# Moving the slot arithmetic of eight pairs of units from VectorE to GpSimd, in a delta-rule attention and mixture-of-experts kernel

## Chip, cores and metric

One core of one Trainium2 chip. The metric is the device time of one execution in microseconds; three runs of the kernel before gave 531.09, 531.88 and 532.16 us, median 531.88 us.

## What is computed

Two stages, in float32. The first is linear attention with a delta rule, for 4 batches and 8 heads, 768 time steps, head dimension 48:

```python
for t in range(S):
    y[:, :, t] = einsum('bhd,bhde->bhe', q[:, :, t], state)
    v_old = einsum('bhde,bhd->bhe', state, k_n[:, :, t])
    state = state + beta_t * einsum('bhd,bhe->bhde', k_n[:, :, t], v[:, :, t] - v_old)
```

The second takes the 3072 rows of that output (384 wide) through a top-1 mixture of 8 experts:

```python
logits = x @ w_gate
expert_idx = argmax(logits, axis=1)          # the first of equals
gate_w = softmax(logits)[arange(N), expert_idx]
out[row] = gate_w[row] * (relu(x[row] @ w1[e]) @ w2[e])   # e = expert_idx[row]
```

## The kernel before

The sequence is cut into 6 blocks of 128 steps; a block of one batch is a **unit**, so there are 24 units, numbered n = 6 blocks x 4 batches in the order in which they are finished. The first part of the kernel is a pipeline over stages t = 0 to 26. In a stage, four units are in flight, each with another quarter of its 128 rows.

The order of the instructions is written out by hand (the program is traced with a manual schedule, and each engine does its instructions in that order). One stage does this:

- `residual(t)`: TensorE multiplies states and earlier corrections (L395, L407) into `ks`, and VectorE subtracts `ks` from the values `v_all` (L414).
- `apply(t)`: TensorE multiplies `v_all` with the inverse of a triangular matrix (L422), and ScalarE copies the result to `u` (L426).
- `finish(n)` for the unit n = t - 3: TensorE starts the output `yp` (L445), makes the state's increment `ku` (L454), VectorE adds it to the state (L458), TensorE completes `yp` (L463), ScalarE copies it to `yt` (L467). In the stage after that, `emit_x` transposes the unit's output into rows of tokens and gate logits (L487 on TensorE, L488 on ScalarE, L489 on VectorE).
- Between these, `beside(t, 0)` to `beside(t, 6)` issue other work, seven portions in a stage: steps of the triangular inverses of later blocks (VectorE, L355 and L359, a product into `tmp` and a subtraction from `lw`, alternating), and steps of the slot arithmetic below, 3, 3, 3, 2, 2, 2 and 2 in the seven portions. The first three portions lie between L414 and L458 of a stage, the other four behind L458.
- `qpart(n)` makes the masked products `pm`: TensorE (L260), two copies by ScalarE (L270), then GpSimd's AFFINE_SELECT over 1024 columns (L271), once in a stage.

**Slot arithmetic** (`emit_slots`, L491 to L565). Two finished units form a pair (the last four units go one by one). Each token must learn its row in `xg`, a table in device memory where the tokens of an expert lie together. On the small arrays [128 tokens, 2 units, 8 experts] VectorE does: the row's maximum (L505), logits minus maximum into `row` (L508), a descending number where that is zero (L513), its maximum (L516), the one-hot `ohb` of the first of equals (L519). Ten steps later TensorE counts (L523, L526: a triangle of ones and ones times `ohb`, into `pp` in PSUM). Then VectorE does seven more: position (L529), the running count `base` (L531), overflow test (L539), its addition (L541), times one-hot (L543), sum over the experts into `sl_all` (L545), cast to integers `sli` (L553). SyncE writes the rows to `xn`, and GpSimd scatters the two units' rows to `xg` with two indirect transfers (L560). ScalarE copies two columns of token numbers into `row` (L511).

The number of the expert (`m2_all`, from L516) is used again only in the part for experts that overflow their 448 rows (L1102 on); in this data that part does not run, and no instruction of it is in the trace.

The second part of the kernel goes over the 8 experts (`ffn`): three products for each matmul (high and low halves of float32), TensorE nearly without a gap from 300 us to the end. The first expert's weights are loaded and split from stage 20 on, and half of its tokens are worked on in the last stages (`early`).

At the start, GpSimd makes constants (`constants()`, L75 to L97): masks, `rev_e`, `base`, `lim`, token numbers.

Of the kernel before, what the change touches and what calls it, by code (L numbers as in the profile page):

```python
# [8 lines left out]
F32 = mybir.dt.float32  # L9
F32R = mybir.dt.float32r  # L10
BF16 = mybir.dt.bfloat16
I32 = mybir.dt.int32
AF = mybir.ActivationFunctionType
ALU = mybir.AluOpType
AX = mybir.AxisListType
# [4 lines left out]
C = 128  # L20
NT = S // C
# [20 lines left out]
def deltanet_moe(ctx, tc, kt_d, qt_d, kn_d, v_d, beta_d, w_gate, w1, w2, out):  # L42
# [13 lines left out]
    ltri = cp.tile([128, 128], BF16, name="ltri")  # L56
    ones = cp.tile([128, 128], BF16, name="ones")
    rev_e = cp.tile([128, E], F32, name="rev_e")
    base = cp.tile([128, E], F32, name="base")
    lim = cp.tile([128, E], F32, name="lim")  # L60
    jump = cp.tile([128, 2, E], F32, name="jump")
# [1 line left out]
    kind_i = cp.tile([128, E], I32, name="kind_i")  # L63
    sl_all = cp.tile([128, B * NT], F32, name="sl_all")
    m2_all = cp.tile([128, B * NT], F32, name="m2_all")
    ids = cp.tile([128, B * NT], F32, name="ids")
    ids2 = cp.tile([128, B * NT, 2], F32, name="ids2")
    zrow = cp.tile([128, ROW], F32, name="zrow")
# [3 lines left out]
    def iota(t, pattern, start, step=0):  # L72
        nc.gpsimd.iota(t, pattern=pattern, base=start, channel_multiplier=step, allow_small_or_imprecise_dtypes=True)

    def constants():  # L75
        nc.gpsimd.memset(esel, 0.0)
        for p in range(NP):
            for a in range(2):

                r = slice(64 * a, 64 * a + D)  # L80
                nc.gpsimd.tensor_copy(esel[r, p, (p + a) % 2 * D:((p + a) % 2 + 1) * D], ident[r, r])
        cmask = lp.tile([128, 128], F32, name="cmask", tag="u", bufs=UB)
        nc.gpsimd.memset(cmask, 1.0)
        nc.gpsimd.affine_select(out=cmask, in_=cmask, compare_op=ALU.is_gt, fill=0.0, base=0,
                                pattern=[[1, 128]], channel_multiplier=-1)
        nc.gpsimd.tensor_copy(ltri, cmask)
        nc.gpsimd.memset(ones, 1.0)
        iota(last_i, [[1, CAP - 128 * NG]], 128 * NG)
        iota(rev_e, [[-1, E]], E)
        iota(base, [[CAP, E]], 0)  # L90
        iota(lim, [[CAP, E]], CAP)
        nc.gpsimd.memset(jump, 0.0)
        for i, g in enumerate((G0, NG)):
            nc.gpsimd.memset(jump[:, i, 0:1], float(128 * g))
        iota(ids, [[-C, B * NT]], int(TOPID), -1)
        nc.gpsimd.memset(ids2, 0.0)
        nc.gpsimd.tensor_copy(ids2[:, :, 0], ids)  # L97
        wv = w_gate.rearrange("(p a r) e -> a r p e", p=NP, a=2)
        for a in range(2):
            for o in range(2):  # L100
                nc.sync.dma_start(out=esel[64 * a:64 * a + D, o::2, 2 * D:], in_=wv[(a + o) % 2, :, o::2])
# [30 lines left out]
    DM2 = 0  # L132
    DEF = 2
    FP = 10
    AH = 3
    TOK = (0, 5, 8, 9, 10)
    PC = (1, 3, 4, 6, 8, 9, 11)
# [82 lines left out]
    def kpart(n):  # L220

        tb, b = n // B, n % B
        kt, gg = kt_t[n] if n < KTL else kg_t[n % KTG], gg_t[n % KSL]
        V, A = nc.vector.tensor_copy, nc.scalar.copy
        if tb == 0:
            if n == 0:
                tiles["dg"] = fp.tile([128, BH, 32], F32, name="dg")
            dg = tiles["dg"]
            db = [psg_[-1].tile([128, NP, 32], F32, name=f"db{b}_0", tag="g"),
                  pss.tile([128, NP, 32], F32, name=f"db{b}_1", tag="y", bufs=YB)]  # L230
            for h in range(H):
                p, a = h // 2, h % 2
                r = slice(64 * a, 64 * a + 64)
                for i in range(NB):
                    t = slice(32 * i, 32 * i + 32)
                    nc.tensor.matmul(db[a][t, p, :], lhsT=kt[r, p, t], rhs=kt[r, p, t], start=True, stop=True,
                                     tile_position=(64 * a, 32 * i), skip_group_check=True)
            V(out=dg[:, b * H:(b + 1) * H:2], in_=db[0])
            A(out=dg[:, b * H + 1:(b + 1) * H:2], in_=db[1])
            yield  # L240
        pg = halves(f"pg{tb}_{b}", kt, kt)
        for a in range(2):
            A(out=gg[:, a:H:2], in_=pg[a])  # L243
        if tb > 0 and b == B - 1:
            for i in range(NB):
                r = slice(32 * i, 32 * i + 32)
                nc.sync.dma_start(out=gd[tb].rearrange("(i n) (r c) -> i r n c", i=NB, r=32)[i],
                                  in_=gg_g[tb % (KSL // B)].rearrange("p b h c -> p (b h) c")[r, :, r])
            tiles[tb]["lg"] = fp.tile([128, 32, 32], F32, name=f"lg{tb}", tag="lg", bufs=3)
            nc.sync.dma_start(out=tiles[tb]["lg"].rearrange("p r c -> p (r c)"), in_=gd[tb])  # L250
        if n >= KTL:
            load_g(n + KTG)
# [177 lines left out]
    def finish(n):  # L430

        tb, b = n // B, n % B
        last = tb == NT - 1
        st, u = st_t[b], uview(n)
        qt, pm = qt_t[n % QTL], pm_t[n % QSL]
        yp = [pss.tile([128, NP // 2, C], F32, name=f"yp{tb}_{b}_0", tag="y", bufs=YB),
              psg_[-1].tile([128, NP // 2, C], F32, name=f"yp{tb}_{b}_1", tag="g")]

        def place(h, m):
            o = 64 * ((h // 2 + h) % 2)  # L440
            return yp[h // 2 % 2][o:o + m, h // 4, :]

        for h in range(H):
            r = slice(64 * (h % 2), 64 * (h % 2) + 64)
            nc.tensor.matmul(place(h, 64), lhsT=st[r, h // 2, r], rhs=qt[r, h // 2, :], start=(h < 4), stop=True,  # L445
                             tile_position=(r.start, 64 * ((h // 2 + h) % 2)), skip_group_check=True)
        yield
        if not last:
            ku = pss.tile([112, NP, D], F32, name=f"ku{tb}_{b}", tag="y", bufs=YB)
            for h in range(H):  # L450

                m = 64 if h % 2 == 0 else D
                kn = tiles[tb][b]["kn"].rearrange("t h d -> t (h d)")[:, h * D:h * D + m]
                nc.tensor.matmul(ku[64 * (h % 2):64 * (h % 2) + m, h // 2, :], lhsT=kn, rhs=u[:, h, :],  # L454
                                 start=True, stop=True, skip_group_check=True)
            for a in range(2):
                r = slice(64 * a, 64 * a + D)
                nc.vector.tensor_tensor(out=st[r, :, r], in0=st[r, :, r], in1=ku[r], op=ALU.add)  # L458
            if n + NB_ < NN - B:
                load_ku(n + NB_)  # L460
        yield
        for h in range(H):
            nc.tensor.matmul(place(h, D), lhsT=u[:, h, :], rhs=pm[:, h, :],  # L463
                             start=False, stop=True, skip_group_check=True)
        yt = lp.tile([128, NP, C], F32, name=f"yt{tb}_{b}", tag="yt", bufs=2)
        for o in range(2):
            nc.scalar.copy(out=yt[:, o::2], in_=yp[o])  # L467
        yield
        w = 1 if n >= NN - W1 else 2
        if n % w == 0:  # L470
            tiles["row", n // w, w] = (rp if n < NN - 2 else xq_[0]).tile([128, 2 if n < NN - 2 else 1, ROW], F32, name=f"row{tb}_{b}", tag="row", bufs=2)
            tiles["rl", n // w, w] = lp.tile([128, 2, E], F32, name=f"rl{tb}_{b}", tag="rl", bufs=2)
        row, rl = tiles["row", n // w, w], tiles["rl", n // w, w]
        row, rl = row[:, 0:w], rl[:, 0:w]
        emit_x(n, yt, row[:, n % w], rl[:, n % w])
        if n % w == w - 1:
            fine.append(emit_slots(tb, b - w + 1, w, row, rl))

    def st_view(b, p):
        t = st_t[b][:, p, :]  # L480
# [10 lines left out]
    def emit_slots(tb, b, w, row, rl):  # L491
# [3 lines left out]
        def small(nm, shape, dt=F32):  # L495
            return lp.tile(shape, dt, name=f"{nm}{tb}_{b}", tag=f"{nm}{w}", bufs=2)
# [15 lines left out]
        oh = small("oh", [128, w, E])  # L512
        V.scalar_tensor_tensor(out=oh, in0=lm, scalar=0.0, in1=both(rev_e), op0=ALU.is_ge, op1=ALU.mult)  # L513
        yield
        m2 = m2_all[:, cols]
        V.tensor_reduce(out=m2, in_=oh, axis=AX.X, op=ALU.max)  # L516
        yield
        ohb = small("ohb", [128, w, E], BF16)
        V.tensor_tensor(out=ohb, in0=oh, in1=wide(m2), op=ALU.is_ge)  # L519
        for _ in range(FP if w > 1 else 3):  # L520
            yield
# [41 lines left out]
            load_main(0, 0, G0)  # L563
        if tb * B + b + w == NN - DEF:
            load_main(0, G0, NG)  # L565

    def run(gen, steps=1):

# [534 lines left out]
    def small(nm, shape=(128, E), dt=F32):  # L1103
        return op.tile(list(shape), dt, name=nm)
# [8 lines left out]
    tsi = small("tsi", (128, B * NT), I32)  # L1113
    nc.vector.tensor_scalar(out=tm, in0=sl_all, scalar1=BIG, scalar2=-BIG, op0=ALU.is_ge, op1=ALU.mult)
    nc.vector.tensor_tensor(out=ts_, in0=sl_all, in1=tm, op=ALU.add)
    nc.vector.tensor_scalar(out=tm, in0=m2_all, scalar1=-float(N - CAP), scalar2=float(E * (N - CAP)),
                            op0=ALU.mult, op1=ALU.add)
    nc.vector.tensor_tensor(out=ts_, in0=ts_, in1=tm, op=ALU.add)
# [123 lines left out]
```

## Time and profile before

| | |
|---|---|
| median of 3 runs | 531.88 us (531.09 to 532.16) |
| the profiled execution: its time / its span | 529.1 us / 527.4 us |
| granted TensorE clock, mean over the span | 0.949 of full speed |
| TensorE matmul busy | 468.1 us (89%) |
| VectorE busy | 350.7 us (66%) |
| ScalarE busy | 268.4 us (51%) |
| GpSimd busy | 97.0 us (18%) |

The span runs from the first to the last instruction of the profiled execution; the 1.7 us between span and time lie outside of it. Busy times are unions: two overlapping instructions of an engine are counted once. In the busy map, VectorE is at nine tenths or more from 50 to 210 us in nearly every slice, and TensorE from 280 us on.

### The profile page before, as it was taken

The page shows a single profiled execution, that of the slowest core. Times are in us where ns is not written, and L with a number is a line of the kernel's source. Part 1 is how long each engine was busy: PE and PEld are TensorE (multiplying, and loading weights), DVE is VectorE, ACT ScalarE, POOL GpSimd, SP SyncE. Part 2 cuts the span into 40 slices and gives each one's busy share as a digit, 9 for nine tenths or more (in the row PEclk, how much of TensorE's full clock was granted, in tenths as well). Part 3 has the DMA queues.
Part 4 walks back from the last instruction along what each step waited for, and adds up shares of the span by engine and source line. Part 5 has one row for each costly group of instructions (what it writes and reads, how often), then busy time and mean ns, then how long its engine had stood idle before and what let it go on. Part 6 is the DMA issues. An engine that isn't in the chain of part 4 may idle for free. (4 is left out here: it accounts for less than half of the span.)

```text
span 527.4 us, 17531 instructions
## 1 busy us (share of the span) xinstructions
PE 468.1 (89%) x7212; PEld 429.8 (81%) x7212; DVE 350.7 (66%) x1135; ACT 268.4 (51%) x614; POOL 97.0 (18%) x125
## 2 busy tenths in 40 slices
PE   6866678998869888988889999999999999999995
PEld 4755667887758766877679889999999999999995
DVE  3999998899998999736654386636372837445330
ACT  2542346877747565755644255635354636344320
POOL 7001012033222212313230211020202020110202
PEclk9976879999998897998999999999999999999999
DMA  5878789588595654594452156655373746453001
GB/s 139 214 259 232 240 223 289 134 237 230 127 272 160 188 150 143 180 287 128 152 155 75 66 170 206 186 166 164 114 226 116 214 126 208 140 163 108 33 2 44
DMA packets 66061, 87.88 MB, mean 167 GB/s; under 512 B 26426, under 2 KB 50768, under 8 KB 65969
## 3 DMA queue, kind: packets, MB, share of 16 engines
q1 hardware_dynamic: 62512, 77.01, 49.8%
q0 software_dynamic: 3456, 9.57, 5.0%
q8 instruction: 67, 1.10, 0.9%
q14 instruction: 26, 0.20, 0.1%
HBM read 60.24 MB, written 23.56 MB: 159 GB/s over the span
## 5 line engine op out<-in xcount | busy, mean ns | idle before, releaser
L668 PE MATMUL y<-w2h,hx 128*128 128x384 f32 x352 | 94.2, 342 | 0.4 <-PEq L1041 0.4
L593 DVE TENSOR_TENSOR w2l<-w2r,w2h 128x768 fp32r<-128x768 f32 x32 | 31.3, 981 | 70.0 <-ACT w2h L592 69.7
L355 DVE TENSOR_TENSOR tmp<-lg,lw 128x192 f32<-128x192 f32 (+28 forms) x269 | 74.0, 310 | 2.8
L359 DVE TENSOR_TENSOR lw<-lw,tmp 128x192 f32<-128x192 f32 (+28 forms) x269 | 69.6, 294 | 0.5
L671 POOL DMA_INDIRECT out_dram<-yo,idx x32 | 30.6, 958 | 202.4 <-ACT yo L1014 129.0
L426 ACT COPY u<-ks 32x384 f32<-32x384 f32 x96 | 45.1, 470 | 39.3 <-PE ks L422 28.4
L668 PEld LDWEIGHTS y<-w2h,hx 128*128 128x128 f32 x352 | 64.2, 188 | 0.7 <-issue 0.7
L668 PE MATMUL y<-w2l,hx 128*128 128x384 f32 x176 | 59.5, 338 | 0.0
L657 PE MATMUL h<-xl,w1h 128*128 128x384 f32 (+1 forms) x168 | 57.6, 343 | 0.2 <-DVE xl L593 0.2
L657 PE MATMUL h<-xh,w1h 128*128 128x384 f32 (+1 forms) x168 | 57.6, 343 | 0.0
L657 PE MATMUL h<-xh,w1l 128*128 128x384 f32 (+1 forms) x168 | 57.5, 342 | 0.0
L271 POOL TENSOR_SCALAR_AFFINE_SELECT pm<-pm 128x1024 f32<-128x1024 f32 x24 | 27.3, 1138 | 130.0 <-ACT pm L270 130.0
L422 PE MATMUL ks<-v_all,wt 32*32 32x48 f32 x1536 | 28.7, 213 | 24.8 <-DVE v_all L414 22.2
L660 ACT ACTIVATE hx<-h 128x448 fp32r<-128x448 f32 (+1 forms) x64 | 32.8, 518 | 33.4 <-PE h L657 32.8
L395 PE MATMUL ks<-st,kt 128*32 128x96 f32 x768 | 46.7, 257 | 1.8 <-issue 1.8
L422 PEld LDWEIGHTS ks<-v_all,wt 32*32 32x32 f32 x1536 | 23.9, 112 | 29.7 <-DVE v_all L414 24.8
L661 DVE SCALAR_TENSOR_TENSOR hx<-h,hx 128x448 fp32r<-128x448 f32 (+1 forms) x64 | 37.0, 588 | 15.3 <-ACT hx L660 15.0
L1014 ACT ACTIVATE yo<-y,gt 128x384 f32<-128x384 f32 x21 | 12.2, 582 | 66.8 <-PE y L668 50.5
L243 ACT COPY gg<-pg 128x512 f32<-128x512 f32 x48 | 25.8, 588 | 32.6 <-PE pg L260 32.6
L395 PEld LDWEIGHTS ks<-st,kt 128*32 128x32 f32 x768 | 34.7, 113 | 5.5 <-issue 2.6
L560 POOL DMA_INDIRECT xg<-row,sli x24 | 26.1, 1089 | 69.1 <-DVE sli L553 39.8
L260 PE MATMUL pq<-qt,kt 64*128 64x128 f32 x384 | 32.3, 303 | 3.2 <-issue 1.9
(164 smaller groups left out, 955.0 us busy)
## 6 DMA issues: line engine op xcount, KB each, us to landing
w1r<-in_w_dram SPq DMA_DIRECT2D x24, 512.0 KB
w2r<-in_w_dram SPq DMA_DIRECT2D x32, 384.0 KB
kt<-in_kt_dram SPq DMA_DIRECT2D x24, 256.0 KB
qt<-in_qt_dram SPq DMA_DIRECT2D x24, 256.0 KB
xg<-zrow SPq DMA_DIRECT2D x7, 788.0 KB
kg<-in_kt_dram SPq DMA_DIRECT2D x17, 256.0 KB
xr<-xg SPq DMA_DIRECT2D x7, 591.0 KB
xn<-row SPq DMA_DIRECT2D x10, 394.0 KB
```

Of the source, the lines that this page charges most:

```text
L260: nc.tensor.matmul(pg[a][:, p], lhsT=kt[r, p], rhs=xt[r, p], start=True, stop=True, tile_position=(64 * a, 0), skip_group_check=True)
L355: nc.vector.tensor_tensor(out=x, in0=lg[:, r0:r1, c:c + 1].broadcast_to([128, r1 - r0, b - a]), in1=lw[:, c:c + 1, a:b].broadcast_to([128, ...
L359: nc.vector.tensor_tensor(out=lw[:, r0:r1, a:b], in0=lw[:, r0:r1, a:b], in1=x, op=ALU.subtract)
L395: nc.tensor.matmul(ks[32 * q:32 * q + 32, 2 * p:2 * p + 2, :], lhsT=kt_t[n % KTL][:, p, 32 * q:32 * q + 32], rhs=st_view(n % B, p), start= ...
L422: nc.tensor.matmul(ks[r, h, :], lhsT=tiles[n // B]["wt"][r, n % B * H + h, :], rhs=vn[r, h, :], start=True, stop=True, tile_position=(32 * ...
L426: nc.scalar.copy(out=uview(n)[r], in_=ks[r])
L593: nc.vector.tensor_tensor(out=lo, in0=src, in1=hi.bitcast(F32), op=ALU.subtract)
L657: nc.tensor.matmul(ps, lhsT=w[:, d, fs], rhs=x_[:, d], start=(n == 0), stop=(n == len(terms) - 1))
L660: nc.scalar.activation(out=hh, in_=ps, func=AF.Relu)
L661: nc.vector.scalar_tensor_tensor(out=hl, in0=ps, scalar=0.0, in1=hh.bitcast(F32), op0=ALU.max, op1=ALU.subtract)
L668: nc.tensor.matmul(ps, lhsT=h(f)[h_], rhs=w2[w][:, f, :], start=(n == 0), stop=(n == len(terms) - 1))
L671: nc.gpsimd.indirect_dma_start(out=out, out_offset=bass.IndirectOffsetOnAxis(ap=idx, axis=0), in_=yo, in_offset=None, bounds_check=N - 1, ...
```

## The change

For the pairs whose units lie below 16 (eight pairs) the slot arithmetic is done by a new function, `pool_slots`. VectorE keeps the row's maximum alone. GpSimd does the rest on the same small arrays. It has no sum or maximum along a row in this code: a sum over 8 experts is three additions of halves (8 to 4 to 2 to 1). The first of equals is found with powers of two: the zeros of logits minus maximum are weighted by 256, 128, ..., 2, summed, the sum is halved, and only the largest weight is above half of the sum. GpSimd does not read PSUM here, so ScalarE copies the counts `pp` to SBUF (`ct`) first.

Other edits: `m2_all` is no longer filled in the pipeline but worked out from the kept one-hots (`oh_all`) in the overflow part; the 4 KB tile `dg` of the start joins the ring of the `lg` tiles; eight more one-column memsets make the weights.

```diff
+    pow_e = cp.tile([128, E], F32, name="pow_e")
+    oh_all = cp.tile([128, B * NT, E], BF16, name="oh_all")
...
+        for e in range(E):
+            nc.gpsimd.memset(pow_e[:, e:e + 1], float(2 << (E - 1 - e)))
...
+    PG = 16
...
-                tiles["dg"] = fp.tile([128, BH, 32], F32, name="dg")
+                tiles["dg"] = fp.tile([128, BH, 32], F32, name="dg", tag="lg", bufs=3)
...
-            fine.append(emit_slots(tb, b - w + 1, w, row, rl))
+            fine.append((pool_slots if n < PG else emit_slots)(tb, b - w + 1, w, row, rl))
...
-        m2 = m2_all[:, cols]
+        m2 = small("m2", [128, w])
...
-        ohb = small("ohb", [128, w, E], BF16)
+        ohb = oh_all[:, cols]
...
+    def pool_slots(tb, b, w, row, rl):
+        G = nc.gpsimd
...
+        def total(x, out):
+            y = small("s", [128, w, 6])
+            for k, y in (4, y[:, :, 0:4]), (2, y[:, :, 4:6]), (1, out.unsqueeze(2)):
+                G.tensor_tensor(out=y, in0=x[:, :, 0:k], in1=x[:, :, k:2 * k], op=ALU.add)
+                x = y
...
+        nc.vector.tensor_reduce(out=mx, in_=rl, axis=AX.X, op=ALU.max)
+        yield
+        lm = row[:, :, DM:DM + E]
+        G.tensor_tensor(out=lm, in0=rl, in1=wide(mx), op=ALU.subtract)
+        cols = slice(b * NT + tb, (b + w - 1) * NT + tb + 1, NT)
+        nc.scalar.copy(out=row[:, :, DM + E:ROW], in_=ids2[:, cols])
+        oh = small("oh", [128, w, E])
+        G.tensor_scalar(out=oh, in0=lm, scalar1=0.0, scalar2=None, op0=ALU.is_ge)
+        yield
+        G.tensor_tensor(out=oh, in0=oh, in1=both(pow_e), op=ALU.mult)
+        yield
+        m2 = small("m2", [128, w])
+        total(oh, m2)
+        yield
+        G.tensor_scalar(out=m2, in0=m2, scalar1=0.5, scalar2=None, op0=ALU.mult)
+        G.tensor_tensor(out=oh, in0=oh, in1=wide(m2), op=ALU.subtract)
+        ohb = oh_all[:, cols]
+        G.tensor_scalar(out=ohb, in0=oh, scalar1=0.0, scalar2=None, op0=ALU.is_gt)
+        for _ in range(FP):
+            yield
...
+        ct = small("ct", [128, w + 1, E])
+        nc.scalar.copy(out=ct, in_=pp)
+        pos, ovr = small("pos", [128, w, E]), small("oh", [128, w, E])
+        G.tensor_tensor(out=pos, in0=ct[:, 0:w], in1=both(base), op=ALU.add)
+        G.tensor_tensor(out=base, in0=base, in1=ct[:, w], op=ALU.add)
+        yield
+        G.tensor_tensor(out=ovr, in0=pos, in1=both(lim), op=ALU.subtract)
+        G.tensor_scalar(out=ovr, in0=ovr, scalar1=0.0, scalar2=BIG, op0=ALU.is_ge, op1=ALU.mult)
+        yield
+        G.tensor_tensor(out=pos, in0=ovr, in1=pos, op=ALU.add)
+        G.tensor_tensor(out=pos, in0=pos, in1=ohb, op=ALU.mult)
+        yield
+        sl = sl_all[:, cols]
+        total(pos, sl)
+        yield
+        sli = rp.tile([128, w], I32, name=f"sli{tb}_{b}", tag=f"sli{w}", bufs=2)
+        G.tensor_copy(sli, sl)
...
+    mo = small("mo", (128, B * NT, E))
+    nc.vector.tensor_tensor(out=mo, in0=oh_all, in1=rev_e.unsqueeze(1).broadcast_to([128, B * NT, E]), op=ALU.mult)
+    nc.vector.tensor_reduce(out=m2_all, in_=mo, axis=AX.X, op=ALU.max)
```

The matmuls into `pp`, the write of `xn` and the two scatters to `xg` stand in `pool_slots` as in `emit_slots`. Behind the counts there are five steps up to the cast in place of seven.

## Rows read from the trace of the kernel before

**Rows 1.** Busy time by stretch; columns: stretch, engines' busy us (instructions), clock, DMA, GB/s.
```profile
95.00:215.00 120.00, 104.51 (x2914) 89.78 (x2909) 112.21 (x453) 80.02 (x240) 28.42 (x26) 0.93 0.64 182
...
220.00:230.00 10.00, 9.68 (x326) 8.36 (x327) 6.06 (x20) 7.32 (x22) 3.19 (x4) 1.00 0.64 205
```

**Rows 2.** Waits, 90 to 230 us: who waited for whom, us in total, times, longest.
```profile
PE ks L422 <- DVE v_all L414: 7.5, 6, 2.0
...
DVE st L458 <- PE ku L454: 1.6, 4, 0.6
```

**Rows 3.** Timeline of VectorE, first half of the third pair's arithmetic: start, us, instruction.
```profile
127.98 0.56 DVE L414 TENSOR_TENSOR v_all<-v_all,ks 128x384 f32<-128x384 f32 x1
...
130.16 0.18 DVE L508 TENSOR_TENSOR row<-rl,mx 128x16 f32<-128x16 f32 x1
130.37 0.18 DVE L513 SCALAR_TENSOR_TENSOR oh<-row,rev_e 128x16 f32<-128x16 f32 x1
130.46 0.42 DVE L355 TENSOR_TENSOR tmp<-lg,lw 128x256 f32<-128x256 f32 x1
...
131.26 0.16 DVE L516 TENSOR_REDUCE m_all<-oh 128x2 f32<-128x16 f32 x1
131.46 0.17 DVE L519 TENSOR_TENSOR ohb<-oh,m_all 128x16 bf16<-128x16 f32 x1
131.55 0.71 DVE L458 TENSOR_TENSOR st<-st,ku 48x192 f32<-48x192 f32 x2
```

**Rows 4.** Timeline of VectorE, second half, one stage later.
```profile
137.59 0.56 DVE L414 TENSOR_TENSOR v_all<-v_all,ks 128x384 f32<-128x384 f32 x1
...
139.06 0.17 DVE L529 TENSOR_TENSOR pos<-base,pp 128x16 f32<-128x16 f32 x1
139.26 0.16 DVE L531 TENSOR_TENSOR base<-base,pp 128x8 f32<-128x8 f32 x1
139.34 0.17 DVE L539 TENSOR_TENSOR ovr<-pos,lim 128x16 f32<-128x16 f32 x1
139.43 0.18 DVE L489 TENSOR_REDUCE rl<-xp 128x8 f32<-128x32 f32 x1
139.54 0.18 DVE L541 SCALAR_TENSOR_TENSOR pos<-ovr,pos 128x16 f32<-128x16 f32 x1
139.75 0.17 DVE L543 TENSOR_TENSOR pos<-pos,ohb 128x16 f32<-128x16 f32 x1
139.96 0.17 DVE L545 TENSOR_REDUCE sl_all<-pos 128x2 f32<-128x16 f32 x1
140.05 0.39 DVE L355 TENSOR_TENSOR tmp<-lg,lw 128x231 f32<-128x231 f32 x1
140.36 0.16 DVE L553 CAST sli<-sl_all 128x2 int32<-128x2 f32 x1
140.43 0.71 DVE L458 TENSOR_TENSOR st<-st,ku 48x192 f32<-48x192 f32 x2
```

**Rows 5.** Timelines of VectorE and of GpSimd around one masking of pm.
```profile
67.70 1.13 DVE L355 TENSOR_TENSOR tmp<-lg,lw 128x175 f32<-128x175 f32 x1
...
69.10 0.34 DVE L359 TENSOR_TENSOR lw<-lw,tmp 128x175 f32<-128x175 f32 x1
...
99.88 0.56 DVE L414 TENSOR_TENSOR v_all<-v_all,ks 128x384 f32<-128x384 f32 x1
```

**Rows 6.** Timeline of GpSimd at the same two places.
```profile
67.55 1.09 POOL L271 TENSOR_SCALAR_AFFINE_SELECT pm<-pm 128x1024 f32<-128x1024 f32 x1 [17.54 <-ACT pm L270]
...
99.80 1.09 POOL L271 TENSOR_SCALAR_AFFINE_SELECT pm<-pm 128x1024 f32<-128x1024 f32 x1 [9.87 <-ACT pm L270]
```

**Rows 7.** GpSimd's groups by line: a small copy; busy us, mean ns.
```profile
L97 POOL COPY ids<-ids 128x24 f32<-128x24 f32 x1 | 0.2, 207 | 0.1
```

**Rows 8.** Timeline of TensorE: the third pair's counts.
```profile
134.36 0.18 PE L523 MATMUL pp<-ohb,ltri 128*128 128x16 bf16 x1
```

**Rows 9.** Timeline of ScalarE: the token numbers' copy.
```profile
129.16 0.20 ACT L511 COPY row<-ids 128x4 f32<-128x4 f32 x1
```

More of the change, by code (lines that the diff above doesn't have):

```diff
@@ L565, in emit_slots, with small, wide, both @@
             load_main(0, G0, NG)
+    def pool_slots(tb, b, w, row, rl):
+        G = nc.gpsimd
+        def small(nm, shape, bufs=1):
+            return lp.tile(shape, F32, name=f"{nm}{tb}_{b}", tag=f"g{nm}", bufs=bufs)
+        def wide(t):
+            return t.unsqueeze(2).broadcast_to([128, w, E])
+        def both(t):
+            return t.unsqueeze(1).broadcast_to([128, w, E])
+        def total(x, out):
[3 more added lines that the diff above has]
+                x = y
+        mx = small("mx", [128, w])
+        nc.vector.tensor_reduce(out=mx, in_=rl, axis=AX.X, op=ALU.max)
[18 more added lines that the diff above has]
+            yield
+        pp = pss.tile([128, w + 1, E], F32, name=f"pp{tb}_{b}", tag="y", bufs=YB)
+        nc.tensor.matmul(pp[:, 0:w, :], lhsT=ltri, rhs=ohb, start=True, stop=False, skip_group_check=True)
+        for j in range(1, w + 1):
+            for i in range(j):
+                nc.tensor.matmul(pp[:, j, :], lhsT=ones, rhs=ohb[:, i], start=False, stop=(i == j - 1),
+                                 skip_group_check=True)
+        ct = small("ct", [128, w + 1, E])
[15 more added lines that the diff above has]
+        G.tensor_copy(sli, sl)
+        yield
+        nc.sync.dma_start(out=xn.rearrange("(b t p) c -> t p b c", b=B, p=C)[tb, :, b:b + w], in_=row)
+        for j in range(w):
+            for _ in range((4, 6)[j]):
+                yield
+            nc.gpsimd.indirect_dma_start(out=xg, out_offset=bass.IndirectOffsetOnAxis(ap=sli[:, j:j + 1], axis=0),
+                                         in_=row[:, j], in_offset=None, bounds_check=E * CAP - 1, oob_is_err=False)
```

## The prediction

> **What bounds the kernel now.** I read the busy times by stretch first. From 95 to 215 us VectorE is busy for 112.2 of 120 us, more than any other engine, and GpSimd for 28.4 [rows 1]. That stretch holds seven of the eight pairs. The eighth lies in 220 to 230 us, where the inverses are done: VectorE is busy for 6.06 of 10 us, TensorE for 9.68, so there VectorE's work isn't the limit.
>
> Next I asked whether the others wait for VectorE. From 90 to 230 us TensorE's apply waited six times, 7.5 us, for the subtraction L414; in the other direction VectorE's state update L458 waited four times, 1.6 us, for TensorE's `ku` [rows 2]. VectorE sets the pace mostly, but not everywhere, so I looked at where in a stage the removed instructions lie. A stage has two stretches on VectorE: from L414 to L458 and from L458 to the next L414. The timeline of the third pair shows all eleven removed instructions in the first kind, four of them ahead of one L458, seven ahead of the next [rows 3, 4]. This decides what their removal can give: behind L414 there is a chain over other engines (apply on TensorE, `u` on ScalarE, `ku` on TensorE) that ends in L458. Where VectorE's own work is shorter than that chain, VectorE waits, and less work on it brings nothing. The shortest such stretch in the 14 of the seven pairs is the one of rows 4: 137.59 to 140.43, 2.84 us. I take 2.84 us as the length of the chain.
>
> **What is removed.** I price an instruction by the distance to the next start, not by its 0.17 us, because starts follow closer where instructions don't depend on each other. First half: 0.21 (L508), 0.09 (L513), 0.20 (L516), 0.09 (L519), together 0.59 us [rows 3]. Second half: 0.20, 0.08, 0.09 (L529, L531, L539), 0.21, 0.21, 0.09 (L541, L543, L545), 0.07 (L553), together 0.95 us [rows 4]. So a pair takes 1.54 us of VectorE, and seven pairs 10.8 us, 9% of the stretch.
>
> What of it shortens a stage, over the 14 stretches: three of them end in a wait for `ku` (the fourth wait of rows 2 is the eighth pair's), and the one of rows 4 is already at 2.84 us, so these four give nothing. That is two first halves and two second halves. The first half of the third pair, 3.57 us long (127.98 to 131.55, rows 3), can give its 0.59 us, as 2.98 is still above 2.84. The nine others are 3.4 to 5.4 us long and can give theirs, but for one of 3.80 us that already holds 0.36 us of idle time; I count 0.3 for it. Sum: first halves 4 x 0.59 + 0.3 = 2.7 us, second halves 5 x 0.95 = 4.8 us, **7.5 us** together. The eighth pair: nothing. Bounds: 4 us, if the chain is 3.5 us in most stages, and 10.8 us.
>
> **What is added on GpSimd.** Nineteen instructions for a pair, nine up to the one-hot and ten behind the counts, all of them reading SBUF. The trace has none of these forms. The nearest row is a copy of 24 columns, 0.207 us [rows 7]; with a second input I take 0.23 us, and about 0.3 us from one to the next as each depends on the one ahead. A pair then takes some 5.7 us, in about 18 us of two stages. GpSimd has room for it, since it is busy for 28 of 120 us.
>
> What it costs VectorE is the largest unknown. The masking of `pm` shows that the two engines hinder each other: a product of 128x175 that started 0.15 us behind an AFFINE_SELECT of 1.09 us took 1.13 us, and an instruction of the same width soon after took 0.34 [rows 5, 6]. It lost 0.79 us, and it ran as if begun at 68.49, 0.15 us ahead of the masking's end at 68.64. L414, which has one input in PSUM, took 0.56 us beside another masking [rows 5, 6], as elsewhere. So a GpSimd instruction holds up VectorE's instructions with two SBUF inputs, for its own length less 0.15 to 0.3 us. For one of 0.23 us that leaves 0 to 0.08 us; I take 0.02, as next to the lower end since nearly every VectorE start overlaps its predecessor anyway. Bounds: 0 and the whole 0.23. With 7 x 19 = 133 instructions, 0.02 us makes **2.7 us** lost. Nothing hides it: the GpSimd chains begin near L458 and near the counts, so they run mostly beside the stretch from L458 to L414, which is filled with L355 and L359.
>
> The Trainium skill, "SBUF — State Buffer", section "Who interferes with whom", calls this an exclusive lock: the one of the two that starts first keeps the shared ports for its whole instruction, and the other fully blocks; two SBUF inputs on VectorE conflict with a GpSimd instruction that reads SBUF. On which instructions conflict, rows 5 and 6 agree with it. On the length they show 0.15 us less than the whole instruction. By the page the sum's second term would be up to 133 x 0.23 = 30.6 us in place of 2.7, and the change a clear loss.
>
> **The wait added on TensorE.** The counts now wait for GpSimd's one-hot. From the first removed instruction at 130.16 to the counts at 134.36 there are 4.2 us [rows 3, 8], and some 0.6 us less when the first half gets shorter. Nine instructions at 0.3 us are 2.7 us; if each also waits 0.15 us for VectorE's ports, 4.1 us. So the counts will often just wait. Behind them TensorE's queue holds `pg`, the transposes `xp` and then the apply, which waits for L414 in many stages anyway [rows 2]. I take 1 us in all, between 0 and 6 (0.9 us in each of seven pairs).
>
> **Other edits.** ScalarE's eight copies of `pp` at about 0.2 us each, like the copy of the token numbers [rows 9], make 1.6 us; ScalarE is busy for 80 of 120 us [rows 1], so I take 0, at most 1.6 if its copies become the chain. They also free the buffer of `pp` earlier than VectorE's reading did at 139.06 and 139.26 [rows 4]. The scatters come two steps earlier on GpSimd, without effect on the path; the write of `xn` stands at the same place in SyncE's queue relative to them. Eight memsets at the start lie behind the constants that others need, `dg`'s ring hands each buffer on as before, and the overflow part doesn't run: 0 for these three, up to about 1 us either way for the moved start.
>
> **Sum.** -7.5 + 2.7 + 1 = -3.8 us, say -4. The profiled execution has 529.1 us, 2.8 below the median of 531.88, so it becomes 525; against the median the forecast is **528.0 us**. What is saved before 215 us passes on to the end, because the later stages start from it and nothing there has a fixed time.
>
> **Rivals.**
> - *The ports cost as much as the removal gives.* Place: the stretch from L458 to L414. The point from which it decides is (7.5 - 1)/133 = 0.05 us lost for each GpSimd instruction. At 0.1 us the loss is 13.3, the net +6.8, the time about 538.5; at the whole 0.23 us it would be near 556. For it: nineteen instructions replace eleven, and two thirds of VectorE's time there is L355 and L359. Against it: the 0.15 us or more that the masking didn't charge. Chance 0.23.
> - *No change.* The removed instructions lie ahead of L458, and the chain that ends there holds in most stretches, or the late counts take back what VectorE gives: 4 - 2.7 - 1, about 531.6. For it: waits for `ku` in four places already. Against it: VectorE has 7.8 us of idle time in 120 us. Chance 0.15.
> - *The full gain.* Small GpSimd instructions slip between VectorE's, and the counts don't wait: -7.5, and some more where the freed `pp` helps, so 523 to 525. Chance 0.19.
> - The forecast, a gain of 2 to 6 us: 0.43.
>
> **How the numbers follow.** A measurement of this kernel can tell about 0.2% from no change, 1.1 us. Faster by more: 0.43 + 0.19, less a little for the forecast's lower edge, 0.60. Within: 0.15. Slower: the first rival and late counts at 6 us, 0.25. The range must reach both ways: down to 523.0 (the full gain with a little more), up to 537.0 (a loss of 0.09 us for each instruction). What is left out is the loss of whole instructions, and a gain of 10.8 us. The likeliest case's own range is 526 to 530. TensorE's clock averages 0.93 of full speed in the stretch [rows 1]; other gaps may move when it falls, by a microsecond or so.
>
> **What would show it.** Right: 88 fewer VectorE instructions and 152 more on GpSimd besides the memsets; small GpSimd instructions of 0.2 to 0.3 us; the stage from one L414 to the next about 0.3 us shorter between 95 and 215 us; L355 and L359 with a mean hardly above before. Wrong, first rival: L355 and L359 longer by several microseconds in total. Wrong, late counts: TensorE waiting at L523 for GpSimd's one-hot in most pairs, and VectorE idle at L414 after it. Wrong, no change: idle time ahead of L458 grown by as much as was removed.

## The result, and the profile after

Thirteen runs of each kernel on one chip gave a median of 526.84 us (520.84 to 532.29) for the changed kernel and 530.75 us (529.22 to 532.67) for the one before. The ratio is 0.9892, with a 95% interval of 0.9862 to 0.9923: **1.1% faster**, by 0.8 to 1.4%. Each ratio here leaves out the executions more than 1.5% above the fastest of the same kernel, which are three of the changed kernel (529.47 to 532.29 us) and none of the one before, so the ratio of the two medians, 0.9926 or 0.7% faster, belongs beside it.

The two profiled executions are 2.1 us apart (529.1 and 526.98 us). The busy time by stretch of the changed kernel, first the stretch that answers to [rows 1], then the whole execution:

```profile
95.00:215.00 120.00, 105.52 (x3001) 91.27 (x3000) 107.69 (x396) 84.02 (x259) 63.83 (x152) 0.94 0.64 186
...
0.00:526.00 526.00, 464.26 (x7212) 426.79 (x7212) 341.90 (x1047) 268.54 (x622) 137.98 (x285) 0.94 0.56 167
```

VectorE has 88 instructions less than the 1135 of before and is busy for 341.90 us in place of 350.7. GpSimd has 160 more than 125: the 152 of the arithmetic and eight memsets. Its groups by line (busy us, mean ns of one, idle before), a cheap and a dear one among them, and the small copy of [rows 7]:

```profile
L611 POOL TENSOR_SCALAR oh_all<-oh 128x16 bf16<-128x16 f32 x8 | 3.4, 429 | 0.7
...
L609 POOL TENSOR_TENSOR oh<-oh,m 128x16 f32<-128x16 f32 x8 | 2.2, 280 | 0.7
...
L636 POOL CAST sli<-sl_all 128x2 int32<-128x2 f32 x8 | 1.7, 208 | 0.5
...
L101 POOL COPY ids<-ids 128x24 f32<-128x24 f32 x1 | 0.2, 205 | 0.1
```

The forms lie between 0.21 and 0.43 us. GpSimd's busy time rose by 41.0 us, which is 0.27 us for each of the 152. The first pair's nine instructions up to the one-hot, in GpSimd's timeline:

```profile
92.58 0.25 POOL L596 TENSOR_TENSOR row<-rl,mx 128x16 f32<-128x16 f32 x1 [3.63 <-DVE mx L593]
92.92 0.27 POOL L600 TENSOR_SCALAR oh<-row 128x16 f32<-128x16 f32 x1
93.28 0.26 POOL L603 TENSOR_TENSOR oh<-oh,pow_e 128x16 f32<-128x16 f32 x1
...
95.08 0.26 POOL L611 TENSOR_SCALAR oh_all<-oh 128x16 bf16<-128x16 f32 x1
```

From 92.58 to 95.08 there are eight steps, 0.31 us each, and the one-hot is there 2.8 us after the start.

On VectorE three groups tell the story. Before (busy, mean, idle ahead and its releaser):

```profile
L355 DVE TENSOR_TENSOR tmp<-lg,lw 128x192 f32<-128x192 f32 (+28 forms) x269 | 74.0, 310 | 2.8
L359 DVE TENSOR_TENSOR lw<-lw,tmp 128x192 f32<-128x192 f32 (+28 forms) x269 | 69.6, 294 | 0.5
...
L458 DVE TENSOR_TENSOR st<-st,ku 48x192 f32<-48x192 f32 x40 | 14.0, 350 | 6.2 <-PE ku L454 5.7
```

After, where the same lines are L360, L364 and L463:

```profile
L364 DVE TENSOR_TENSOR lw<-lw,tmp 128x192 f32<-128x192 f32 (+28 forms) x269 | 73.3, 308 | 0.5
L360 DVE TENSOR_TENSOR tmp<-lg,lw 128x192 f32<-128x192 f32 (+28 forms) x269 | 72.5, 304 | 2.9
...
L463 DVE TENSOR_TENSOR st<-st,ku 48x192 f32<-48x192 f32 x40 | 14.0, 350 | 13.1 <-PE ku L459 12.8
```

The two inverse lines take 145.8 us in place of 143.6. Little of that growth lies beside the small GpSimd instructions. Two pairs of inverse steps that run beside the chain shown above, from 92.42 us:

```profile
92.42 0.50 DVE L364 TENSOR_TENSOR lw<-lw,tmp 128x180 f32<-128x180 f32 x2
92.96 0.50 DVE L360 TENSOR_TENSOR tmp<-lg,lw 128x168 f32<-128x168 f32 x2
```

The same steps before, while GpSimd does nothing (from 89.94 to 99.80 us):

```profile
94.70 0.49 DVE L359 TENSOR_TENSOR lw<-lw,tmp 128x180 f32<-128x180 f32 x2
95.23 0.49 DVE L355 TENSOR_TENSOR tmp<-lg,lw 128x168 f32<-128x168 f32 x2
```

Taken one by one from the traces (each instruction against the median of the same line and shape where GpSimd does nothing near it), the 109 inverse instructions that ran beside small GpSimd instructions alone are longer by 0.2 us in all. The other 2.0 us lie in the instructions that an AFFINE_SELECT touches: 38 of them, 14.1 us too long, where before 34 were 12.1 us too long.

The idle time ahead of the state update grew by 6.9 us. VectorE's busy time fell by 8.8 us, and its other idle times changed both ways and nearly cancel (ahead of L494 3.3 us more, ahead of L419 1.9 less), so the span became only 2.1 us shorter. The waits from 90 to 217 us say where it stands (total, times, longest; TensorE's wait for the subtraction answers to the first of [rows 2]):

```profile
PE ks L427 <- DVE v_all L419: 10.2, 9, 3.2
DVE st L463 <- PE ku L459: 6.6, 4, 2.7
...
PE pp L615 <- POOL oh_all L611: 0.6, 2, 0.4
```

Before, the state update waited in the same stretch as follows:

```profile
DVE st L458 <- PE ku L454: 1.4, 3, 0.6
```

TensorE's waits for the subtraction grew from 7.5 to 10.2 us, so VectorE still holds it up. The counts waited twice for GpSimd's one-hot, 0.6 us in all. Not all of VectorE's waiting comes from the change: the longest of the four follows a gap in TensorE's own queue, in the middle of an apply, for which the profile shows no releaser ("issue"), in TensorE's timeline:

```profile
93.32 0.69 PE L427 MATMUL ks<-v_all,wt 32*32 32x48 f32 x19 [1.93 <-issue]
```

Such gaps of 0.35 us and more sum to 11.6 us between 10 and 300 us in the profile of before (twelve of them) and to 11.2 us after (eight), at partly other places. They add to what one profile differs from the next, and the medians are the better evidence for the size.

### The profile page after: what moved, and what is told of

Read it like the earlier page. It is cut to its first block, busy times and chain, and to the rows that moved or that the text cites. A ratio compares the mean times of both kernels' runs of the same rounds, so it can differ in the third digit from the quotient of the medians.

```text
span 525.3 us, 17583 instructions
## 1 busy us (share of the span) xinstructions
PE 464.3 (88%) x7212; PEld 426.8 (81%) x7212; DVE 341.9 (65%) x1047; ACT 268.5 (51%) x622; POOL 138.0 (26%) x285
## 5 line engine op out<-in xcount | busy, mean ns | idle before, releaser
L360 DVE TENSOR_TENSOR tmp<-lg,lw 128x192 f32<-128x192 f32 (+28 forms) x269 | 72.5, 304 | 2.9
L364 DVE TENSOR_TENSOR lw<-lw,tmp 128x192 f32<-128x192 f32 (+28 forms) x269 | 73.3, 308 | 0.5
L427 PE MATMUL ks<-v_all,wt 32*32 32x48 f32 x1536 | 27.1, 212 | 29.2 <-DVE v_all L419 24.2
L427 PEld LDWEIGHTS ks<-v_all,wt 32*32 32x32 f32 x1536 | 22.6, 111 | 34.0 <-DVE v_all L419 27.4
L1092 ACT ACTIVATE yo<-y,gt 128x384 f32<-128x384 f32 x21 | 12.2, 582 | 66.9 <-PE y L746 50.8
L400 PE MATMUL ks<-st,kt 128*32 128x96 f32 x768 | 45.3, 253 | 1.1 <-issue 1.0
L400 PEld LDWEIGHTS ks<-st,kt 128*32 128x32 f32 x768 | 33.5, 111 | 4.5 <-issue 1.4
L671 DVE TENSOR_TENSOR w1l<-w1r,w1h 128x1024 fp32r<-128x1024 f32 x24 | 29.4, 1224 | 7.3 <-ACT w1h L670 7.1
L265 PE MATMUL pq<-qt,kt 64*128 64x128 f32 x384 | 30.6, 291 | 3.6 <-issue 2.3
```

What stands on the lines that cost most here:

```text
L265: nc.tensor.matmul(pg[a][:, p], lhsT=kt[r, p], rhs=xt[r, p], start=True, stop=True, tile_position=(64 * a, 0), skip_group_check=True)
L360: nc.vector.tensor_tensor(out=x, in0=lg[:, r0:r1, c:c + 1].broadcast_to([128, r1 - r0, b - a]), in1=lw[:, c:c + 1, a:b].broadcast_to([128, ...
L364: nc.vector.tensor_tensor(out=lw[:, r0:r1, a:b], in0=lw[:, r0:r1, a:b], in1=x, op=ALU.subtract)
L400: nc.tensor.matmul(ks[32 * q:32 * q + 32, 2 * p:2 * p + 2, :], lhsT=kt_t[n % KTL][:, p, 32 * q:32 * q + 32], rhs=st_view(n % B, p), start= ...
L427: nc.tensor.matmul(ks[r, h, :], lhsT=tiles[n // B]["wt"][r, n % B * H + h, :], rhs=vn[r, h, :], start=True, stop=True, tile_position=(32 * ...
L671: nc.vector.tensor_tensor(out=lo, in0=src, in1=hi.bitcast(F32), op=ALU.subtract)
```

## The experiments

The theory: the move gains what VectorE's eleven instructions took wherever the chain from L414 to L458 leaves room for it (7.5 us), and costs about 0.02 us of VectorE for each GpSimd instruction through the shared ports, and about 1 us of late counts. Rivals: the gain comes from the side edits; the ports cost nothing, or several times more.

Twelve kernels ran in three groups (e0 to e3, e4 to e7, e8 to e11), each group on one chip with its own runs of before (medians 530.65, 531.53 and 530.26 us). The changed kernel itself ran in the second group alone (e6_after).

**Nothing moved (e0_pg0).**

```diff
-    PG = 16
+    PG = 0
```

> The changed kernel with the bound of the move at unit 0, so that no pair is moved: what is left is the kept one-hots, the eight memsets and the ring for dg. Theory (the gain comes from VectorE's removed instructions): within 0.2% of before, 529.7 to 531.8 us at a median of before of 530.75. Rival (the gain comes from the side edits or from where instructions and buffers lie): faster by 0.5% or more, below 528.

Measured: median 531.61 us, ratio 1.0001 (0.9953 to 1.0048). The side edits and the new places of code and tiles change nothing that shows; a gain of 0.5% lies just at the interval's edge. The idle time ahead of the state update is 6.9 us here, near before's 6.2.

**All added, nothing removed (e3_keep).** VectorE's eleven instructions are done too, beside GpSimd's; the small tiles on VectorE have one buffer in place of two. The core of the edit:

```diff
+        V.tensor_tensor(out=dl, in0=rl, in1=wide(mx), op=ALU.subtract)
         G.tensor_tensor(out=lm, in0=rl, in1=wide(mx), op=ALU.subtract)
...
+        V.tensor_tensor(out=dp_, in0=both(base_d), in1=pp[:, 0:w, :], op=ALU.add)
         nc.scalar.copy(out=ct, in_=pp)
...
+        V.tensor_tensor(out=base_d, in0=base_d, in1=pp[:, w, :], op=ALU.add)
...
+        V.tensor_copy(di, ds)
```

> The changed kernel, but VectorE does its eleven instructions for each moved pair as well, at the steps where they stood, on scratch tiles that nobody reads (base_d for base). So nothing is removed and all of GpSimd's work is added. Theory: slower than before by the two costs, 2.7 for the ports and 0 to 1 for late counts, 533.5 to 534.5, and 6 to 8 us above the changed kernel. Rival, the ports cost nothing: as before, 530.7. Rival, 0.1 us an instruction: 13 us above before; whole instructions of 0.23 us: some 30 us above before.

Measured: median 534.51 us, ratio 1.0058 (1.0015 to 1.0100): 3.1 us slower than before, by 0.8 to 5.3. This is the run that separates the two terms. What is added costs about 3 us, and 133 instructions at 0.1 us are excluded. What is removed is worth the distance to the changed kernel: 534.51 against 526.84 and 526.28 us in its two comparisons, 7.7 to 8.2 us (across chips, and with at least the 2.2 us either way of e3_keep's own interval). In its trace the inverse instructions that an AFFINE_SELECT touches are 14.2 us too long (12.1 before), those beside small GpSimd instructions alone 0.3 us. The idle time ahead of its state update is back where it was:

```profile
L465 DVE TENSOR_TENSOR st<-st,ku 48x192 f32<-48x192 f32 x40 | 14.0, 350 | 5.2 <-PE ku L461 5.0
```

**The two halves alone (e1_front, e2_back).** In the first, the part behind the counts is that of `emit_slots`; in the second, the part up to the one-hot is.

```diff
-        G.tensor_tensor(out=pos, in0=ct[:, 0:w], in1=both(base), op=ALU.add)
...
+        V.tensor_tensor(out=pos, in0=both(base), in1=pp[:, 0:w, :], op=ALU.add)
...
```

> Only the first half (up to the one-hot, nine GpSimd instructions) is moved for the eight pairs; the second half stays on VectorE and reads PSUM. Theory: 2.7 us gained, 7 x 9 x 0.02 = 1.3 us lost to the ports and up to 1 us to late counts, so 0.5 to 1.5 us faster than before, about 529.5. Rival, ports at 0.1 us an instruction: 6.3 us lost, 3.5 us slower than before. Rival, the freed buffer of the counts makes the gain: no change here.

> Only the second half (behind the counts, ScalarE's copy and ten GpSimd instructions) is moved; the first half stays on VectorE. Theory: 4.8 us gained, 1.4 us lost, 3 to 3.5 us faster than before, about 527.5; no late counts. Rival, ports at 0.1 us: 7 us lost, 2 us slower than before. Rival, the freed buffer of the counts makes the gain: the whole 4 us here.

Measured: first half 530.11 us, ratio 0.9933 (0.9881 to 0.9986); second half 529.08 us (one of its twelve executions took 1066.60 us, for which nothing here shows a reason), ratio 0.9953 (0.9912 to 0.9994). By the ratios each alone is faster by an amount whose interval runs from under 1 us to 5 or 6 us, and together, 1.1%, they are the whole; by the medians of all executions they are 0.5 and 1.6 us below before (0.9990 and 0.9970), so a gain of either half alone is not clear of the noise. The rival that makes each half 2 us or more slower (0.1 us an instruction) has both against it. That the second half gives everything is not excluded: its interval reaches 0.9912. Which half gives more can't be told: the medians say the second, as expected, the ratios the first.

**Twenty more GpSimd instructions, reading or writing (e4_read20, e5_write20).** They stand between the one-hot and the counts; the small tiles that stay on VectorE have one buffer in place of two, to make room.

```diff
-        for _ in range(FP):
+        for i_ in range(FP):
+            for k_ in range(2):
+                sc = lp.tile([128, w, E], F32, name=f"sc{tb}_{b}_{i_}_{k_}", tag=f"gsc{k_}", bufs=1)
+                G.tensor_tensor(out=sc, in0=oh, in1=both(pow_e), op=ALU.mult)
             yield
```

In e5_write20 the last of these lines is `G.memset(sc, 0.0)`.

> The changed kernel unchanged, so that the other kernels of this group have it on the same chip. Every theory: a ratio of about 0.99 to before, as in the first comparison.

> The changed kernel with twenty more GpSimd products of the same small size for each moved pair, into scratch, two at each of the ten steps between the one-hot and the counts, so beside the stretch from L458 to L414. They read SBUF as the real ones do. 140 of them lie in the seven pairs. Theory (0.02 us of VectorE lost for each): 3 us above the changed kernel, and 3 us above the kernel with memsets. Rival, the ports cost nothing: as the changed kernel. Rival, 0.1 us: 14 us above it; the whole 0.23 us: some 30 us above it.

> The same with twenty memsets of the same scratch tiles in place of the products: as many more instructions on GpSimd, that only write. Theory and all rivals on the read ports: as the changed kernel, within 1 us. A rival in which GpSimd's in-order queue delays something (the masking of pm, the scatters): 2 us or more above it, here as well as with the products.

Measured, on one chip: the changed kernel again (e6_after) 526.28 us, ratio 0.9873 (0.9805 to 0.9941); with products 530.74, ratio 1.0000 (0.9952 to 1.0049); with memsets **520.04**, ratio 0.9809 (0.9743 to 0.9875), all six runs between 518.83 and 525.46. The products cost 4.5 us by the medians, in the range of the theory's 3, but most of it is not the price that the theory gave them. In the profiled execution, at 535.25 us the longest of its twelve, the inverse lines take 149.9 us in place of 145.8 after:

```profile
L364 DVE TENSOR_TENSOR lw<-lw,tmp 128x192 f32<-128x192 f32 (+28 forms) x269 | 75.4, 315 | 0.5
L360 DVE TENSOR_TENSOR tmp<-lg,lw 128x192 f32<-128x192 f32 (+28 forms) x269 | 74.5, 312 | 2.9
```

Of these 4.1 us, 1.1 lie beside small GpSimd instructions alone (1.3 us over 184 inverse instructions, 0.2 in the profile after), under 0.01 us for each product; 2.9 lie in the instructions that an AFFINE_SELECT touches (17.0 us too long). And the counts came late: TensorE waited three times for the one-hot, 9.3 us in all, for another reason than the arithmetic's length. In the timelines of GpSimd and TensorE:

```profile
116.76 1.09 POOL L645 DMA_INDIRECT xg<-row,sli  x1 [3.63 <-DMA xg<-row,sli]
117.85 0.26 POOL L596 TENSOR_TENSOR row<-rl,mx 128x16 f32<-128x16 f32 x1
...
120.31 0.26 POOL L611 TENSOR_SCALAR oh_all<-oh 128x16 bf16<-128x16 f32 x1
```
```profile
120.62 0.17 PE L618 MATMUL pp<-oh_all,ltri 128*128 128x16 bf16 x1 [3.59 <-POOL oh_all L611]
```

The second scatter of the pair before stood ahead of the next pair's arithmetic in GpSimd's queue and waited 3.63 us for the first scatter's landing; TensorE waited 3.59 us for the one-hot in turn.

The kernel with memsets was the faster one, which neither theory nor rival held; it rests on six executions of each, and the intervals of the two ratios overlap. Its inverse lines take 70.0 and 71.4 us, 4.4 us less than after and 2.2 less than before, although all 152 reading instructions are there. The difference lies beside the maskings: the instructions that an AFFINE_SELECT touches are 9.5 us too long, where they were 13.8 in e6_after, 14.1 after and 12.1 before. Its unexplained gaps on TensorE sum to 5.8 us in place of 11.2. Three kernels asked why.

**One buffer, and nothing else (e8_slim).** 

```diff
-            return lp.tile(shape, dt, name=f"{nm}{tb}_{b}", tag=f"{nm}{w}", bufs=2)
+            return lp.tile(shape, dt, name=f"{nm}{tb}_{b}", tag=f"{nm}{w}", bufs=1)
```

> The changed kernel with one buffer in place of two for the small tiles of the slot arithmetic that stays on VectorE, as the two kernels with twenty extra instructions have it, and nothing else. It asks why the kernel with memsets was 6 us below the changed one. Theory (the memsets shift the maskings and scatters in GpSimd's queue): as the changed kernel, a ratio of 0.985 to 0.993. Rival (where tiles lie in SBUF makes it): a ratio of about 0.981, as with the memsets.

Measured: 526.98 us, ratio 0.9961 (0.9926 to 0.9997), the medians' ratio 0.9938. The rival's 0.981 is excluded: not the tiles' places. But the expected 0.985 to 0.993 was missed as well.

**The same number of memsets at the start (e9_early160).**

```diff
+        for i_ in range(160):
+            sc = lp.tile([128, 2, E], F32, name=f"sc_{i_}", tag=f"gsc{i_ % 2}", bufs=1)
+            nc.gpsimd.memset(sc, 0.0)
         wv = w_gate.rearrange("(p a r) e -> a r p e", p=NP, a=2)
```

> The same with 160 memsets in one block on GpSimd behind the constants, before 26 us, and none beside the moved arithmetic: as many more instructions, but no shift of anything later. Theory (shift): as the changed kernel, 0.985 to 0.993. Rival (more GpSimd instructions move the times at which instruction code is loaded, and TensorE waits less for its own): about 0.981.

Measured (with one buffer too): 527.61 us, ratio 0.9987 (0.9955 to 1.0019), the medians' ratio 0.9950. Not the number of GpSimd's instructions as such; they could still shift code loading where they stand among the others, which this run doesn't test. Here too the expected 0.985 to 0.993 was missed, and the interval doesn't reach the 0.9892 of the changed kernel. As the changed kernel did not run on this chip, no run shows whether these edits cost something or its gain is smaller here.

**The memsets in the kernel before (e10_before_mem).**

```diff
-        for _ in range(FP if w > 1 else 3):
+        for i_ in range(FP if w > 1 else 3):
+            for k_ in range(2 if tb * B + b < 16 else 0):
...
+                nc.gpsimd.memset(sc, 0.0)
             yield
```

> The kernel before, its arithmetic on VectorE, with the same twenty memsets on GpSimd for each of the eight pairs between the one-hot and the counts. If the memsets help whatever the arithmetic does: 1% below before. If they help only the moved arithmetic (theory: they hold the maskings and scatters back behind it): as before, within 0.3%.

Measured (with one buffer too): 531.66 us, ratio 1.0032 (0.9997 to 1.0067). They don't help the kernel before; its instructions beside maskings are 12.2 us too long with them, 12.1 without. That a shift of maskings and scatters is the cause fits all three, and the 4.4 us less beside maskings, but no run here shifts these alone: it stays open.

**Inverses moved forward (e7_spend).**

```diff
-    SPEND = (0.8, 0.8, 0.8, 0.85, 0.85, 0.85, 0.85)
+    SPEND = (1.0, 1.0, 1.0, 0.7, 0.7, 0.7, 0.7)
```

> The changed kernel with the inverses' steps of a stage moved forward: portions of 1.0 each in the first three places of a stage (between L414 and L458 of before) and 0.7 in the other four, in place of 0.8 and 0.85, the same sum. Theory (what was removed lies ahead of a state update that waits for TensorE, so part of it became idle time there): the idle time ahead of the state update is filled, 2 to 3 us below the changed kernel. Rival (the gain is used up already, VectorE's total is what counts): as the changed kernel, within 1 us.

Measured, on the chip of e6_after: 525.59 us, ratio 0.9865 (0.9789 to 0.9941), against 526.28 and 0.9873. The idle time ahead of the state update did fall, from 10.0 us in e6_after to this:

```profile
L463 DVE TENSOR_TENSOR st<-st,ku 48x192 f32<-48x192 f32 x40 | 14.0, 349 | 5.3 <-PE ku L459 5.0
```

The time did not follow, or by less than these runs can tell: with six executions of each and intervals of about 4 us either way, the 2 to 3 us that were expected are neither shown nor excluded. Filling that gap doesn't return the whole 7 us that became idle there.

**The first scatter earlier (e11_scatter).**

```diff
-            for _ in range((4, 6)[j]):
+            for _ in range((0, 10)[j]):
```

> The changed kernel with the first scatter of a pair issued right behind the cast, in place of four steps later, and the second at the step where it was. In the kernels with extra instructions the second scatter, waiting for the first one's landing, stood in GpSimd's queue ahead of the next pair's arithmetic, and TensorE then waited up to 4 us for the one-hot. Theory (late counts are 0 to 1 us in the changed kernel): 0 to 1 us below it. Rival (late counts are a good part of its cost, and of its spread): 2 us or more below it, and fewer slow executions.

Measured: 529.26 us, ratio 1.0021 (0.9986 to 1.0056), the medians' ratio 0.9981. Not faster, and by its interval not as fast as the changed kernel in its own comparisons. TensorE's wait for the one-hot is 0.2 us in its profile and 0.6 in the one after, so late counts are no large part of the changed kernel's cost. Whether the earlier scatter takes back the gain, or the chip has a part in it, is open: on this chip none of three small variants of the changed kernel reached its 1.1%.

The version that beats both kernels is the one with twenty memsets: 520.04 us against 526.28 of the changed kernel on the same chip, six executions of each. It rests on timing that isn't understood.

## Why the prediction was right, point by point

- **Direction and size.** 528.0 us was forecast for a median of 531.88, a ratio of 0.9927; 0.9892 (0.9862 to 0.9923) was measured, and 0.9926 by the medians. The likeliest case came about. That it was met so closely is in part luck, as the second term shows.
- **What is removed, 7.5 us.** Between e3_keep and the changed kernel lie 7.7 to 8.2 us (across chips). The fourteen stretches from the subtraction to the state update sum to 58.9 us before, 55.0 in the profile after and 52.0 in that of e6_after: 3.9 and 6.9 us less. The stages that hold them (from the subtraction at 90.54 to that at 219.73 before) became 0.18 and 0.30 us shorter each, where about 0.3 was forecast; so the other stretches, up to the next subtraction, grew by 1.5 and 2.7 us in all, where the prediction put the costs. The step that mattered, to count an instruction only where the chain from the subtraction to the state update leaves room, is borne out by the idle time that appeared ahead of L463, and the chain's length of 2.84 us by the shortest stretches of the profile after. Two rows of its timeline on VectorE, 138.00 to 140.80:

```profile
138.00 0.56 DVE L419 TENSOR_TENSOR v_all<-v_all,ks 128x384 f32<-128x384 f32 x1
...
140.80 0.72 DVE L463 TENSOR_TENSOR st<-st,ku 48x192 f32<-48x192 f32 x2 [0.82 <-PE ku L459]
```

  This is the stretch of [rows 4], 2.84 us long before and 2.80 now: its seven instructions went, and it is as long as ever. What became idle was undercounted: 10.8 - 7.5 = 3.3 us were written off, and the waits for `ku` up to 217 us grew from 1.4 us in three to 6.6 in four, the gap on TensorE at 93 us among them (5.0 in five in e6_after). Nor does all of it pass on to the end: the subtraction at 219.73 us came 3.7 us earlier after, the end of the span 2.1.
- **Ports, 2.7 us.** The inverse lines grew by 2.2 us, and all costs together, without any gain, are 3.1 us (0.8 to 5.3) against the 3.7 of the sum. The size came out by luck, though: 0.02 us for each small instruction is not what the traces show. Beside small instructions alone the inverses lost 0.2 us in all, 0.002 us for each of the 84 small ones that ran there, so that the bound of 0 was the nearer one. The rest of the growth lies in instructions that an AFFINE_SELECT touches, which the prediction didn't count among the costs; whether small ones close behind a masking have a part in it is open. The Trainium skill's rule ("SBUF — State Buffer", "Who interferes with whom": the second of two conflicting instructions blocks for the whole of the first) is no price for short instructions here. By an estimate from it, 133 instructions of 0.27 us would have cost up to 36 us, several times what the removal gives.
- **Late counts, 1 us.** Two waits, 0.6 us in the profile after. The dangerous form of it, in e4_read20, was not the arithmetic's length, as the prediction put it, but the scatter that waits ahead of it in GpSimd's queue.
- **GpSimd's instructions.** 0.23 us with 0.3 us from one to the next were taken; 0.27 and 0.31 were found.
- **Side edits, 0.** e0_pg0: a ratio of 1.0001.

The split between the halves (-1 and -3.4 us) and the nothing for the eighth pair were not settled.

## What to carry to other kernels

Work can be taken from a saturated engine and still not shorten the path: look for the chain that ends at the next wait of that engine, and count only what lies in stretches longer than it. A slower engine with idle time can be the right place for short dependent instructions, if what they feed is needed some microseconds later; what it does in order ahead of them, here a scatter that waited for another, decides whether they are in time. A cost that comes out at the right size can still lie elsewhere: look beside which instructions the loss stands. A run in which everything is added and nothing removed prices both terms of such a move at once.

## What the runs showed of the hardware

- GpSimd takes 0.21 to 0.43 us for instructions of two to sixteen elements a partition, and 0.31 us from one to the next in the first pair's dependent chain.
- Short GpSimd instructions that read SBUF cost a stream of two-input VectorE instructions next to nothing: 0.2 us over the 109 that ran beside them alone in the changed kernel, 1.3 us over 184 in e4_read20. The instructions that an AFFINE_SELECT of 1.1 us touches were 12.1 us too long in all before and 14.1 after, 0.8 us in the one of [rows 5].
- TensorE's gaps without a releaser sum to 7.7 to 13.3 us in thirteen of the fourteen profiles, and to 5.8 us in that of e5_write20.
- With twenty memsets a pair, none of which does any work, the changed kernel was 6 us faster (six executions of each on one chip), and the kernel before was not (on another chip).
